# Attention and mixture of experts on one core: a memset one tile later, tables ahead of W2's low parts, another product order and a drain in the half tiles

## Chip, cores and metric

One core of a Trainium2 chip runs the whole program. The metric is device time of one execution in microseconds (us). Before the change the median of three runs is 827.66 us.

## What is computed

Attention with a forget gate (8 batches, 8 heads, 576 positions, 64 numbers a head), whose output is read as 4608 tokens of 512 numbers. Each token then goes to the one of 8 experts that has the largest gate logit:

```python
for e in range(E):
    mask = e_idx == e
    h = np.maximum(x[mask] @ w1[e], 0.0)
    out[mask] = gate_w[mask, None] * (h @ w2[e])
```

W1 is 512x1024 and W2 1024x512 for each expert, all in float32. Which expert a token has is known only on the chip.

## The kernel before, in words

**Two phases.** Attention takes the first 355 us or so; a planner with due times sets its order, and the change doesn't touch it. Its last steps scatter the tokens into a buffer `xs` in DRAM, sorted by expert (indirect DMAs of GpSimd). The expert phase then walks over tiles of `xs`: up to 18 tiles of 256 tokens (`full`, inside `run`), then up to 8 tiles of 128 tokens (`halves`, `half`, `layers_h`), each within an If on a count that is known at run time. In the executions shown here 18 full tiles and 3 half tiles run.

**Which tile comes next.** A tile's expert, its place in `xs` and whether its weights differ from those of the tile ahead are numbers in small integer tables, made by VectorE (DVE) from the token counts. The first four tiles are served by a table made early (`c_taba`). In tile 2 (`t == TABLES`) `other_tables` makes the others: `c_tabb` for the full tiles from the fifth on, `c_tabc` for the half tiles; the last element of each row is written by the CASTs on lines 1123, 1124 and 1130. `self.tabled` holds the names of the last instructions of the tables. The queue of SyncE (SP) reads a row of the table into registers (line 1176) and then issues the loads of that tile: W1 into `raw1` (two DMAs of 1 MB, line 1204, `load_w1`), W2 into `raw2` (two of 1 MB, line 1217, `load_w2`) and the tokens `xg` (line 1196, `load_x`). It does all this in one order, so a row that isn't there yet holds up every load behind it.

**Products in parts.** For accuracy each float32 operand is split: a rounded high part in the type fp32r (`w1h`, `w2h`, `xh`, `hh`), made by ScalarE (ACT), and a low part in bf16, the rest (`w1l`, `w2l`, `xl`, `hl`), made by DVE as original less high part. A product is then three sums: high by high in fp32r, and high by low and low by high in bf16. `products(ks, last, high, *low)` lists them: with `last` true the fp32r products come at the end, else first.

```python
        m = [(k, *x) for x in low for k in ks]
        h = [(k, *high) for k in ks]
        return m + h if last else h + m
```

**A full tile** (`full(t)`) issues the load of the next W1, splits W2 (`split_w2`, lines 1242 and 1243: four quarters of w2h on ACT and of w2l on DVE), loads the next W2, runs layer 1 (`first`), splits the next W1 (`split_w1`, lines 1223 and 1225), turns the next tile's tokens (`prepare`) and runs layer 2 (`second`), whose two halves of 128 tokens are each scaled by DVE into `y` (line 1322) and stored by an indirect DMA of GpSimd (line 1323). In this phase the framework's scheduler sets each engine's order, held only by the data and by `self.order(x, behind)`, which says that x stands behind another instruction on their engine and adds no wait.

**raw1b.** Half tiles use two W1 buffers in turn, `raw1` and `raw1b`. A load is skipped where the expert doesn't change, so GpSimd zeroes `raw1b` (128x4096) once, in tile 3 (`t == TABLES + 1`, line 1490).

**A half tile** (`layers_h`) is written out by hand for TensorE (PE), ACT and DVE (`manual_schedule`): the order in the code is the order on these engines. Layer 2 has 24 products of 128x512 into one bank `py`, in two halves of 12 (i = 0 and 1, four k each). `products` gets i as its `last`: the first half has fp32r first, the second has it last. After the first four products PE turns the second part of h, DVE makes the last quarter of w2l (`quarter_w2(3, False)`, line 1361) and then all four quarters of the next tile's w1l (line 1225). ACT scales the result into `y` (line 1406) and GpSimd stores it (line 1407).

Of the kernel before, what the change touches and what calls it, by code (L numbers as in the profile page):

```python
# [16 lines left out]
I32 = mybir.dt.int32  # L17
# [25 lines left out]
NT = 4608  # L43
# [6 lines left out]
TABLES = 2  # L50
# [17 lines left out]
def upper(ap):  # L68

    n = len(ap.shape)  # L70
    axes = " ".join("abcd"[:n - 1])
    return ap.bitcast(BF16).rearrange(f"{axes} (n two) -> {axes} n two", two=2)[(slice(None),) * n + (1,)]
# [151 lines left out]
class Attn:  # L224
# [741 lines left out]
    def run(self, early, others):  # L966
        self.others = others
        self.own("acc", -1)
        with self.tc.manual_schedule():
            self.setup(*self.begin)  # L970
            for s in self.steps(early).order():
                s["fn"]()
                self.turn_over(BETWEEN.get(s["name"], 0), 256)
# [19 lines left out]
class Moe:  # L993
# [369 lines left out]
    def layers_h(self, t):  # L1363

        nc = self.nc
        xg, xh, xl = self.xgh[t], self.xhh[t], self.xlh[t]
        hb = self.next("hb")
        ph = [self.next("ph") for _ in range(2)]
        m = [self.products(range(4), q, (xh, self.w1h), (upper(xh), self.w1l), (xl, upper(self.w1h))) for q in range(2)]

        def first(q, js):
            for j in js:
                k, x, w = m[q][j]
                nc.tensor.matmul(ph[q], x[:, k, :], w[:, k, q * 512:q * 512 + 512], start=(j == 0), stop=(j == 11))
            if js[-1] == 11:
                nc.scalar.activation(hb[:, q], ph[q], AF.Relu)

        for q in range(2):
            self.quarter_w2(q, True)
            self.quarter_w2(q, False)  # L1380
        first(0, range(12))
        self.quarter_w2(2, True)
        first(1, range(8))
        self.turn_h(hb, 0)
        self.quarter_w2(2, False)
        first(1, range(8, 12))
        self.quarter_w2(3, True)
        if t < 7:
            self.prepare_h(t + 1, "ph")
        py = self.next("py")  # L1390
        m2 = [x for i in range(2) for x in self.products(range(4 * i, 4 * i + 4), i, (self.hh, self.w2h), (upper(self.hh), self.w2l),
                                                         (self.hl, upper(self.w2h)))]

        def second(js):
            for j in js:
                k, h, w = m2[j]
                nc.tensor.matmul(py, h[:, k, 0:P], w[:, k, :], start=(j == 0), stop=(j == len(m2) - 1))

        second(range(4))
        self.turn_h(hb, 1)  # L1400
        self.quarter_w2(3, False)
        if t < 7:
            self.split_w1((t + 1) % 2)
        second(range(4, 24))
        y = self.next("y")
        nc.scalar.activation(y, py, AF.Copy, scale=xg[:, 512:513])
        nc.gpsimd.indirect_dma_start(self.out, bass.IndirectOffsetOnAxis(ap=xg[:, 513:514].bitcast(I32), axis=0), y, None,  # L1407
                                     bounds_check=NT - 1, oob_is_err=False)

    def early(self, acc, pc):  # L1410

# [53 lines left out]
    def run(self, acc, loads, behind, ahead, ranks):  # L1465
        self.load_w1(self.row[0], 0, loads)
        self.load_w2()
        behind = self.split_w1(0, [0], behind, (0, 2))
        behind = self.prepare(0, behind)
        for x in ahead:  # L1470
            self.order(x, behind[1])
        self.split_w1(0, [1, 2, 3], behind, (0, 2))

        def full(t):
            self.load_w1(self.row[t + 1])
            if t + 2 < FULL and t != TABLES:
                self.load_x(t + 2)
            if t == OTHERS:
                self.pads(pc)
            behind = self.split_w2(None if t else ranks)  # L1480
            self.load_w2()
            self.first(t, None if t else ranks, behind)
            self.split_w1(0, behind=(self.relu, behind[3][1]) if t <= OTHERS else None)
            if t + 1 < FULL:
                self.prepare(t + 1, None if t else (behind[3][0], behind[1][1]))
            if t == TABLES:
                self.other_tables(n)
                self.load_x(t + 2)
            if t == TABLES + 1:
                self.order(self.nc.gpsimd.memset(self.raw1[1], 0.0), self.low)  # L1490
            half = self.second(self.xg[t], 2)
            if t == 0:
                self.half_way = half

        for t in range(ALWAYS):
            if t == OTHERS:
                pc = self.px(0)
                n = self.counts(acc, pc, "b", self.half_way)
            full(t)
        nt = self.val(self.row[EARLY], 3, FULL - EARLY, ALWAYS - EARLY, ())  # L1500
        nh = self.val(self.rowh[0], 3, 8, 0, ())
        for h in range(2):
            self.load_xh(h)
        self.prepare_h(0)
        kept = self.kept()
        with self.tc.If(nt >= FULL - EARLY) as most:
            for t in range(ALWAYS, FULL):
                full(t)
            self.halves(nh)
        with most.Else():  # L1510
            self.kept(kept)
            with ExitStack() as nest:
                for t in range(ALWAYS, FULL - 1):
                    nest.enter_context(self.tc.If(nt > t - EARLY))
                    full(t)
            self.halves(nh)
# [92 lines left out]
```

## Time and profile before

| what | us |
|---|---|
| median of three runs | 827.66 |
| the three runs | 827.66, 821.95, 827.77 |
| the profiled execution: its own time | 822.82 |
| the profiled execution: first to last instruction (span) | 820.8 |
| PE busy | 780.6 |
| DVE busy | 622.6 |
| ACT busy | 593.3 |
| GpSimd (POOL) busy | 388.7 |

Times in the views are us from the span's start. A row of the timeline gives start, length, engine, line, operation, what is written and read, how often, and in brackets how long the engine was idle just before and what ended that. An engine name with a q (POOLq, SPq) is that engine's sequencer or DMA queue. A wait is put down to what came last by the profile.

### The profile page before, as it was taken

Reading aid. Unit: us, or ns where it says so; the run is one execution under the profiler, and the core shown is the slowest. Engines: PE = TensorE matmul, PEld = TensorE weight load, DVE = VectorE, ACT = ScalarE, POOL = GpSimd, SP = SyncE. Lnnn points to the kernel's source line nnn. Section 1 sums busy time; section 2 is a strip of 40 time slices with the busy share of each in tenths; the row PEclk is TensorE's granted clock in tenths of the full one; section 3 lists DMA queues with packets and bytes.
Section 4 is the critical chain, followed back from the end, with each engine's and each line's share of the span. In section 5 each row is a group of like instructions: output and inputs, shape, how many; then the busy total and the mean of one; then the engine's idle time right before and its main releaser. Section 6 shows DMA issues by size and latency. Waiting matters only on the chain. (4 is left out here: it accounts for less than half of the span.)

```text
span 820.8 us, 23634 instructions
## 1 busy us (share of the span) xinstructions
PE 780.6 (95%) x9659; PEld 619.1 (75%) x9659; DVE 622.6 (76%) x1178; ACT 593.3 (72%) x799; POOL 388.7 (47%) x376
## 2 busy tenths in 40 slices
PE   8998999999999998899998999999999999999994
PEld 4788888888888887786777777777777767777552
DVE  7888999889898989777887766665656667666494
ACT  5897989798989897685855665655556667666483
POOL 9767989798989886876524011111011010111110
PEclk9999999999999999999999999999999999999998
DMA  5634444445454533262566821101114421115580
GB/s 169 202 118 133 161 150 161 146 139 172 137 172 139 167 115 113 84 235 84 191 208 212 295 72 53 51 27 39 52 53 141 155 67 53 52 62 173 200 294 22
DMA packets 43622, 108.16 MB, mean 132 GB/s; under 512 B 5547, under 2 KB 6123, under 8 KB 43500
## 3 DMA queue, kind: packets, MB, share of 16 engines
q1 hardware_dynamic: 36778, 85.47, 31.2%
q0 software_dynamic: 6704, 21.02, 7.0%
q8 instruction: 80, 1.31, 0.7%
q14 instruction: 42, 0.34, 0.1%
q10 hardware_dynamic: 18, 0.01, 0.0%
HBM read 143.78 MB, written 22.02 MB: 202 GB/s over the span
## 5 line engine op out<-in xcount | busy, mean ns | idle before, releaser
L1323 POOL DMA_INDIRECT out_dram<-y,xg x36 | 50.6, 1405 | 313.1 <-DVE y L1322 286.0
L586 PE MATMUL ps<-X 64*128 64x288 f32 (+5 forms) x1536 | 150.8, 314 | 1.0 <-ACT X L426 1.0
L702 POOL TENSOR_TENSOR Pl<-Pt,Ph 128x1024 f16<-128x1024 f32 (+1 forms) x63 | 142.2, 2264 | 12.9 <-ACT Ph L690 11.6
L1242 ACT CAST w2h<-raw 128x1024 fp32r<-128x1024 f32 x72 | 70.3, 1043 | 86.2 <-PE py L1318 70.4
L1243 DVE TENSOR_TENSOR w2l<-raw,w2h 128x1024 bf16<-128x1024 f32 x72 | 85.0, 1218 | 45.2 <-ACT w2h L1242 45.2
L586 PEld LDWEIGHTS ps<-X 64*128 64x128 f32 (+1 forms) x1536 | 114.3, 181 | 4.0 <-ACT X L426 1.2
L728 PE MATMUL po<-vh,Ph 128*128 128x73 f16 x930 | 101.5, 199 | 3.5 <-DVE lgh L744 3.3
L1225 DVE TENSOR_TENSOR w1l<-raw,w1h 128x1024 bf16<-128x1024 f32 x78 | 96.1, 1243 | 10.8 <-ACT w1h L1223 10.7
L730 PE MATMUL po<-vh,Pl 128*128 128x73 f16 x930 | 101.0, 198 | 1.0 <-DVE Pl L702 1.0
L729 PE MATMUL po<-vl,Ph 128*128 128x72 f16 x930 | 101.3, 197 | 0.0
L1283 PE MATMUL ph<-xh,w1h 128*128 128x256 f32 x576 | 96.3, 299 | 2.7 <-ACT w1h L1223 2.6
L675 ACT ACTIVATE Pt<-ps,lnp 128x576 f32<-128x576 f32 (+1 forms) x96 | 81.6, 865 | 23.4 <-PE ps L586 23.4
L729 PEld LDWEIGHTS <-Ph 128*128 128x128 f16 x960 | 95.1, 99 | 3.0 <-issue 2.9
L728 PEld LDWEIGHTS <-Ph 128*128 128x128 f16 x960 | 94.1, 99 | 4.0 <-DVE lgh L744 1.9
L432 POOL TENSOR_TENSOR X<-raw,X 128x1152 fp32r<-128x1152 f32 x32 | 85.2, 2664 | 24.2 <-ACT X L426 19.7
L730 PEld LDWEIGHTS <-Pl 128*128 128x128 f16 x960 | 94.0, 98 | 1.1 <-DVE Pl L702 1.1
L1318 PE MATMUL py<-w2h,hh 128*128 128x512 f32 x288 | 88.0, 424 | 0.0
L1283 PE MATMUL ph<-xr,w1l 128*128 128x256 bf16 x576 | 87.0, 273 | 0.0
L1283 PE MATMUL ph<-xl,w1h 128*128 128x256 bf16 x576 | 87.0, 274 | 0.0
L1223 ACT CAST w1h<-raw 128x1024 fp32r<-128x1024 f32 x80 | 82.8, 1054 | 4.1 <-DMA raw<-in_w_dram 4.1
L607 DVE TENSOR_REDUCE mt<-ps 128x2 f32<-128x128 f32 (+3 forms) x128 | 81.9, 681 | 3.5 <-PE ps L586 2.6
L1283 PEld LDWEIGHTS ph<-xh,w1h 128*128 128x128 f32 x576 | 77.5, 190 | 7.9 <-ACT w1h L1223 3.1
(307 smaller groups left out, 1699.7 us busy)
## 6 DMA issues: line engine op xcount, KB each, us to landing
raw<-in_w_dram SPq DMA_DIRECT2D x84, 1024.0 KB
raw<-in_qk_dram SPq DMA_DIRECT2D x32, 608.0 KB
vT<-in_vt_dram SPq DMA_DIRECT2D x32, 320.0 KB
xg<-xs SPq DMA_DIRECT2D x18, 514.0 KB
vr<-in_v_dram SPq DMA_DIRECT2D x30, 256.0 KB
raw1b<-in_w_dram SPq DMA_DIRECT2D x4, 1024.0 KB
hxg<-xs SPq DMA_DIRECT2D x5, 257.0 KB
vr<-in_v_dram SPq DMA_DIRECT2D x8, 128.0 KB
```

Source lines behind the costliest of these rows:

```text
L432: e.tensor_tensor(self.two(X[:, 1]), self.two(self.get("raw", p)), self.two(f32(X[:, 0])), ALU.subtract)
L586: self.nc.tensor.matmul(ps[0:m, h, c:c + w], a(r), b(r), start=start, stop=not any(x[0] is ps for x in parts[n + 1:]), skip_group_check=True)
L607: nc.vector.tensor_reduce(mt[:, :, ic:ic + 1], pm[:, :, c0:c0 + w], AX.X, ALU.max)
L702: e.tensor_tensor(self.Pl_t[p % 2][:, :, c], self.exps(p, i), self.Ph_t[p % 2][:, :, c], ALU.subtract)
L728: nc.tensor.matmul(o, Ph[:, c0:c0 + P], vh[:, c, hh, :], start=(c == 0), stop=False)
L729: nc.tensor.matmul(o[:, 1:73], Ph[:, c0:c0 + P], vl[:, c, hh, :], start=False, stop=False)
L730: nc.tensor.matmul(o, Pl[:, c0:c0 + P], vh[:, c, hh, :], start=False, stop=(c == ic))
L1223: x = nc.scalar.copy(self.w1h[a], self.raw1[i][a])
L1225: y = e.tensor_tensor(self.w1l[a], self.raw1[i][a], f32(self.w1h[a]), ALU.subtract)
L1243: y = nc.vector.tensor_tensor(self.w2l[a], self.raw2[a], f32(self.w2h[a]), ALU.subtract)
L1283: y = nc.tensor.matmul(ph[:, i, :], w[:, k, f0:f0 + P], x[:, k, :], start=(j == 0), stop=(j == len(m) - 1))
L1318: x = nc.tensor.matmul(py, h[:, k, c * P:c * P + P], w[:, k, :], start=(j == 0), stop=(j == len(m) - 1))
```

## The change

Four edits. (1) The memset of `raw1b` is issued in tile 4 (`TABLES + 2`) and no longer in tile 3. (2) In tile 3 the four w2l subtractions are ordered behind the last instructions of the tables. (3) In half tiles both halves of layer 2 have their fp32r products first. (4) In half tiles GpSimd gets a `drain` that its order puts ahead of the store.

```diff
@@ layers_h
-        m2 = [x for i in range(2) for x in self.products(range(4 * i, 4 * i + 4), i, (self.hh, self.w2h), (upper(self.hh), self.w2l),
+        m2 = [x for i in range(2) for x in self.products(range(4 * i, 4 * i + 4), 0, (self.hh, self.w2h), (upper(self.hh), self.w2l),
...
-        nc.gpsimd.indirect_dma_start(self.out, bass.IndirectOffsetOnAxis(ap=xg[:, 513:514].bitcast(I32), axis=0), y, None,
-                                     bounds_check=NT - 1, oob_is_err=False)
+        d = nc.gpsimd.drain()
+        x = nc.gpsimd.indirect_dma_start(self.out, bass.IndirectOffsetOnAxis(ap=xg[:, 513:514].bitcast(I32), axis=0), y, None,
+                                         bounds_check=NT - 1, oob_is_err=False)
+        self.order(x, d.ins.name)
@@ run, full(t)
-            behind = self.split_w2(None if t else ranks)
+            behind = self.split_w2(None if t else ranks, self.tabled if t == TABLES + 1 else ())
...
-            if t == TABLES + 1:
+            if t == TABLES + 2:
                 self.order(self.nc.gpsimd.memset(self.raw1[1], 0.0), self.low)
```

On DVE, between the last y of tile 2 (`y_9392`, line 1322) and layer 1 of tile 3, a minus is before and a plus now:

```order
 L1168 SCALAR_TENSOR_TENSOR c_eb<-c_okb,c_ec,c_eb 1x15
-L1243 TENSOR_TENSOR w2l<-raw_9378,w2h 128x1024 x2
 L1123 CAST c_tabb<-c_eb 1x15
 L1129 TENSOR_TENSOR c_chb<-c_eb 1x15
-L1243 TENSOR_TENSOR w2l<-raw_9378,w2h 128x1024 x2
-L1289 SCALAR_TENSOR_TENSOR hl<-ph_9349,hh 128x512
 L1130 CAST c_tabb<-c_chb 1x15
-L1289 SCALAR_TENSOR_TENSOR hl<-ph_9350,hh 128x512
+L1243 TENSOR_TENSOR w2l<-raw_9378,w2h 128x1024 x4
+L1289 SCALAR_TENSOR_TENSOR hl<-ph_9349,hh 128x512
```

The three small instructions of the table stood between the quarters of w2l and behind a hl; now they come first and the four quarters of w2l follow in one run. On GpSimd's queue the memset stood behind the second store of tile 2 and stands behind the second store of tile 3.

On PE, in the first half tile, at the turn from the first to the second half of layer 2 and at its end (`hh`, `hl` high and low part of h; lines between are the same):

```order
 L1397 MATMUL py_9354<-w2h,hl 128x512
+L1397 MATMUL py_9354<-w2h,hh 128x512 x4
 L1397 LDWEIGHTS hh
 L1397 MATMUL py_9354<-w2l,hh 128x512
...
 L1397 MATMUL py_9354<-w2h,hl 128x512
-L1397 MATMUL py_9354<-w2h,hh 128x512 x4
```

Four fp32r products went from the end of the second half to its start; the bf16 products by w2l come four products later. On PE, in the full tile 13 (counted from 0), where its layer 2 opens before the last quarter of its layer 1 (`px` the turned tokens of the next tile, `py` the results):

```order
+L1263 MATMUL px_9344<-cident,xg_63 128x128 x4
 L1263 MATMUL px_9359<-cident,xg_63 128x128 x4
-L1318 MATMUL py_9354<-w2h,hh 128x512 x2
-L1318 LDWEIGHTS hr
-L1318 MATMUL py_9355<-w2l,hr 128x512
-L1318 LDWEIGHTS hr
-L1318 MATMUL py_9355<-w2l,hr 128x512
-L1318 MATMUL py_9354<-w2h,hh 128x512 x2
```

The scheduler gave the full tiles 5 to 13 another interleave: where fp32r and bf16 products stood in pairs by turns, there is now one fp32r product. Counted over these nine tiles the order has 70 changes from fp32r to bf16 before and 45 now, with the same products; tiles 15 and 16, which are the same in both, have 6 each, and tiles 10 and 11 had 8 each before.

## Rows read from the trace of the kernel before

**Rows 1.** The page's part 1: busy us, share of the span, instructions.
```profile
PE 780.6 (95%) x9659; PEld 619.1 (75%) x9659; DVE 622.6 (76%) x1178; ACT 593.3 (72%) x799; POOL 388.7 (47%) x376
```
**Rows 2.** Windows of 30 us, PE alone: us, busy, granted clock, DMA share, GB/s.
```profile
430.00:460.00 30.00, 27.36 (x195) 1.00 0.72 256
...
760.00:790.00 30.00, 29.44 (x142) 1.00 0.60 219
```
**Rows 3.** Waits of PE, whole span: us in total, times, longest.
```profile
PE ph L1283 <- ACT w1h L1223: 2.6, 1, 2.6
...
PE py L1397 <- DVE w2l L1361: 1.8, 3, 0.6
```
**Rows 4.** Timeline from 428 to 447 us, engine by engine.
```profile
446.97 0.51 PE L1283 MATMUL ph<-xh,w1h 128*128 128x256 f32 x2 [2.64 <-ACT w1h L1223]
...
445.88 1.99 ACT L1223 CAST w1h<-raw 128x1024 fp32r<-128x1024 f32 x2 [4.10 <-DMA raw<-in_w_dram]
...
440.63 1.10 SPq L1204 DMA_DIRECT2D raw<-in_w_dram  x2
...
430.63 0.21 DVE L1168 SCALAR_TENSOR_TENSOR c_eb<-c_okb,c_ec,c_eb 1x15 f32<-1x15 f32 x1
...
436.07 3.90 DVE L1130 CAST c_tabb<-c_chb 1x15 int32<-1x15 f32 x1
...
436.39 3.56 POOL L1490 MEMSET raw1b<- 128x4096 f32 x1
```
**Rows 5.** Windows of 2 us: us, granted clock, DMA share, GB/s.
```profile
438.00:440.00 2.00, 1.00 0.00 0
...
444.00:446.00 2.00, 1.00 1.04 400
```
**Rows 6.** Timeline of the first half tile's layer 2, PE and DVE.
```profile
779.82 0.59 PE L1397 MATMUL py<-w2l,hh 128*128 128x512 bf16 x2
780.97 0.59 PE L1397 MATMUL py<-w2l,hh 128*128 128x512 bf16 x2 [0.56 <-DVE w2l L1361]
...
783.22 0.39 PE L1374 MATMUL ph<-w1h,hxh 128*128 128x512 f32 x1
...
779.70 1.21 DVE L1361 TENSOR_TENSOR w2l<-raw,w2h 128x1024 bf16<-128x1024 f32 x1
```
**Rows 7.** Timeline of the last half tile's end, DVE, ACT and POOL.
```profile
806.59 4.62 DVE L1225 TENSOR_TENSOR w1l<-raw1b,w1h 128x1024 bf16<-128x1024 f32 x4
...
809.18 0.69 ACT L1406 ACTIVATE y<-py,hxg 128x512 f32<-128x512 f32 x1 [0.69 <-PE py L1397]
...
784.38 1.94 POOL L1407 DMA_INDIRECT out_dram<-y,hxg  x1 [11.04 <-ACT y L1406]
...
810.14 1.93 POOL L1407 DMA_INDIRECT out_dram<-y,hxg  x1 [10.96 <-ACTq L1526]
```
**Rows 8.** Line 1605, the program's end: ns min/median/max, first and last start.
```profile
L1605 POOLq DRAIN  x3: 51/107/7276, 812.7 to 820.5; - x3
L1605 SPq DRAIN  x3: 7/7/13, 815.3 to 820.2; - x3
```
**Rows 9.** GpSimd's indirect DMAs: count, ns min/median/max, first and last start.
```profile
L836 POOL DMA_INDIRECT xs<-x,rde x40: 915/988/1966, 92.1 to 384.1; - x40
...
L1188 POOL DMA_INDIRECT xs<-c_nobody,c_at x8: 962/1139/1960, 398.5 to 409.6; - x8
...
L1323 POOL DMA_INDIRECT out_dram<-y,xg x36: 984/996/4712, 385.3 to 771.6; - x36
```
**Rows 10.** PE timeline, the last run of products of four full tiles.
```profile
590.54 2.20 PE L1318 MATMUL py<-w2h,hh 128*128 128x512 f32 x8
...
635.65 2.19 PE L1318 MATMUL py<-w2h,hh 128*128 128x512 f32 x8
...
701.70 2.20 PE L1318 MATMUL py<-w2h,hh 128*128 128x512 f32 x8
746.70 2.21 PE L1318 MATMUL py<-w2h,hh 128*128 128x512 f32 x8
```

## The prediction, made before the changed kernel ran

> **What bounds the kernel now.** I read the page's busy line first: PE works 780.6 of 820.8 us [rows 1], so nothing else can be worth much unless it stops PE or lies behind PE's end. Next the windows of PE, to find where it is not full in the expert phase: between 430 and 460 us it lacks 2.64 us, between 760 and 790 us 0.56 us [rows 2]; in the windows between these it is full. The list of PE's waits names both: one of 2.6 us for w1h, and three, 1.8 us in all, for w2l in the half tiles [rows 3]. Then the timelines of these places, and last the rows of the program's end, which no busy share shows: after the last store GpSimd sits in one DRAIN of 7.28 us [rows 8].
>
> The profiled execution took 822.82 us, 2.0 more than its span. The median of the three runs is 827.66, and the three stand at two levels, 822 and 827.7, some 5 us apart; the profile shows one of the lower level, and nothing in one trace says what the other is made of. My sum is made against 822.82; 827.66 less 822.82 is 4.84, which I add for the median's level.
>
> **Edits 1 and 2: the memset and the tables.** The PE wait at 446.97 is for w1h of tile 4; ACT waited for the W1 data, whose load SP issued at 440.63, and the cast began 5.25 us later [rows 4]. SP could not issue it earlier because the row of c_tabb wasn't complete: its last CAST (one partition, 15 numbers) began at 436.07 and took 3.90 us, until the memset's end (436.39 and 3.56, so 439.95) [rows 4]. Two things made it late: four w2l between it and the table's other instructions, and the memset beside it. In the new order the three small instructions follow c_eb, which ended at 430.84 [rows 4], at once, and the memset isn't near. I put the row at 431.2 and SP's load at 432, 8.6 us earlier than 440.63. The DMA engines are free then (0 GB/s as late as 438 to 440, against 400 in 444 to 446) [rows 5], so the data are there near 437.3 by the same 5.25 us, and PE needs w1h at 444.3. The wait of 2.6 us goes. What is late next: nothing I can see; PE then follows its own products. Term: -2.6, bounds -2.6 and 0.
>
> What edit 2 delays are four w2l, by three instructions as small as c_eb with its 0.21 us [rows 4]; PE reads w2l much later. The memset in its new place stands behind the second store of tile 3, while DVE works on w2l, hl and w1l of tile 4. No row shows it beside these. If they wait as the CAST did, DVE loses up to 3.56 us; DVE is 76% busy [rows 1], and the bound for PE is 0 to +2.6 (3.56 less a microsecond of slack, an estimate). I take 0 because hl and xl read PSUM and the row beside it is a cast, another operation; rival B is the other end. The move past SP's queue costs nothing, since SP's order is unchanged. The stores behind the memset wait for y far later.
>
> **Edit 3: products of the half tiles.** PE stops 0.56 us before the third w2l product, because DVE's last w2l began at 779.70 and took 1.21 us [rows 6]. The twelve products take from 779.82 to 783.22 with that wait [rows 6], so 0.24 each without it. With four fp32r products ahead the third w2l product is the seventh and comes at 779.82 and 6 by 0.24, 781.25, after 780.91 when that w2l ends. The wait is covered in all three tiles: 1.8 us in total [rows 3], 0.6 each. One more change from fp32r to bf16 a tile costs 0.03 by the price below, so nothing. The next tile starts 0.6 earlier; I see no other wait of PE in these tiles that would show an engine on the verge of being late.
>
> In the last half tile the gain reaches the end through the store. Its y starts at 809.18, the store at 810.14 and takes 1.93 [rows 7], so it ends at 812.07, 0.86 behind the end of DVE's four w1l (806.59 and 4.62, so 811.21) [rows 7]. The first and the last of the three stores of half tiles take the same [rows 7], while the shortest in full tiles takes 0.98 [rows 9]. So I read it thus: the store gets its turn where one w1l ends and the next begins. Those seams are 1.15 apart (4.62 by four), at 810.05 too. A store that starts 0.6 earlier, at 809.54, meets that seam and ends one w1l sooner: -1.15 in place of -0.6. Term: 2 by -0.6 and -1.15, so -2.3; bounds -2.4 and -1.2 (the store still ends with the w1l).
> The Trainium skill (SBUF — State Buffer, section Who interferes with whom) infers that a tensor_tensor on DVE doesn't hold up the writing of descriptors by GpSimd. By that the last store would win only 0.6 and the sum would be 0.55 smaller; the rows above, 1.93 beside w1l, speak against it.
>
> **The interleave of the full tiles.** It isn't among the edits but follows from them. Tiles 10 and 11 together take 45.11 us (590.54 to 635.65), tiles 15 and 16, with the same products and 4 changes of type fewer, 45.00 (701.70 to 746.70) [rows 10]: 0.028 a change. 25 changes fewer in nine tiles: -0.7, bounds -1.5 and 0 (it could be the order and not the changes).
>
> **Edit 4: the drain.** Cost first. Each new drain runs where GpSimd is idle anyway: 11 us ahead of each store of a half tile [rows 7]. Below 10 us it delays nothing. Now what it may give. At the end the first of three DRAINs of GpSimd must be the long one: it starts at 812.7 and 7.28 us later, at 819.98, the others follow; SP reached its own drain at 815.3 and so had seen every store landed [rows 8]. So GpSimd alone keeps the program open for 4.7 us. What takes 7.28 us there is not the last store, which landed before 815.3. It may be what 87 indirect DMAs since the start (40, 8, 36 and the 3 of the half tiles [rows 7, 9]) left to be tidied up, 0.084 each; there was no drain in between. Then the first new drain does nearly all of it in GpSimd's idle time, the last finds one store, and the end comes by SP's 815.3: -4.6. Or each drain after a store costs the same 7.28: then 0. No row has a drain behind a few DMAs only, so these are the two bounds. I take -4.6, since the landed data leave little else for it to wait for, but hardly above even chance.
>
> **Sum.** -2.6 - 2.3 - 0.7 - 4.6 = -10.2: 812.6 at the profile's level, 817.5 at the median's.
>
> **Rivals.**
> A: the last drain is as long as before, because its length belongs to any drain behind a store. For it: 7.28 us is a long time for bookkeeping that could have been done in idle time. Then -5.6: 822.1 at the median's level, 817.2 at the profile's.
> B: the memset holds DVE in tile 4 as it held the CAST, and what edit 1 wins is lost a tile later: +2.6. For it the CAST's 3.90 us; against it that DVE's work there has slack and other operations. 820.1.
> The Trainium skill (same page and section) says that a two-input operation from SBUF contends only with GpSimd work that reads SBUF, and a memset only writes; by that rule B falls. No row here shows that pair.
> C, slower: the drains in the half tiles run beside DVE's w1l and w2l, and as the stores there take 1.93 and not 0.98, a drain too may take twice its 7.28 there, 14.6 us, each time. The point from which this decides is the 11 us of idle time. From GpSimd's last store of the full tiles (done at 773.3, 11.04 before 784.38 [rows 7]) three rounds of 14.6 and 1.93 end the last store at 822.9 in place of 812.07; with the 3.3 of edits 1, 2 and the interleave taken off, and the last drain as now, +7.5: 835.2. Against it: the idle time would have had to be just too short, and if the backlog theory holds only the first drain is long.
>
> **How the numbers follow.** Forecast 0.50, A 0.36, B 0.10, C 0.04. The predicted time is the forecast's, 817.5. Each case can come at either level, about as likely, since the runs stand two to one and the profiled one at the lower. The forecast spans 812.6 to 817.5, A 817.2 to 822.1, B 815 to 820. With a microsecond at each end for the bounds the range is 811.8 to 823.2; C and about a tenth of the others lie outside. About 1% is what a measurement of this kernel can tell from no change: 8.3 us, so faster means under 819.4. That holds for the forecast but a tenth (0.45), for A at the lower level (0.16) and a little of B: 0.62. Slower needs over 835.9, the upper side of C and what I haven't seen: 0.03. The rest is 0.35.
>
> **What would show it.** Edits 1 and 2: line 1130's CAST as short as its neighbours, SP's W1 load near 432, PE full between 430 and 460. Edit 3: no wait of PE for w2l in half tiles; the last store about 1 us long. Interleave: tiles 5 to 13 a tenth shorter each. Edit 4: POOLq's new DRAINs, the first long, the last short, and the span's end within a microsecond of SP's drain. It is wrong if the last DRAIN keeps its 7 us (A), if hl or w1l of tile 4 takes 3 us beside the memset (B), or if a store of a half tile starts after its y by more than 0.5 us (C).

## The result, and the profile after

| what | before, us | after, us |
|---|---|---|
| median of six runs each | 824.18 | 814.12 |
| lowest and highest of the six | 821.95, 827.77 | 813.42, 818.33 |
| profiled execution: its own time | 822.82 | 813.55 |
| profiled execution: span | 820.8 | 811.8 |

The ratio after to before is 0.988, 95% interval 0.9846 to 0.9914: faster by about ten microseconds. The forecast was 817.5 in 811.8 to 823.2. The profile of the changed kernel answers the steps one by one. First the page's busy line (columns as in [rows 1]) and the windows of PE (as in [rows 2]):

```profile
PE 780.1 (96%) x9659; PEld 619.9 (76%) x9659; DVE 618.5 (76%) x1178; ACT 593.5 (73%) x799; POOL 385.1 (47%) x376
```
```profile
430.00:460.00 30.00, 30.00 (x221) 1.00 0.78 272
760.00:790.00 30.00, 29.88 (x146) 1.00 0.61 217
```

PE does the same work as before, 780.1 against 780.6 us [rows 1]; both gaps of [rows 2] are closed. The 0.12 us that is missing in the second window is a small new wait, and a later one of the same kind stands in the list of PE's waits, which has no row for w1h (line 1223) and none for w2l (line 1361) any more:

```profile
PE ph L1374 <- DVE w1l L1225: 0.2, 1, 0.2
```

The timeline from 430 to 440 us shows why the first gap closed:

```profile
430.43 0.16 DVE L1130 CAST c_tabb<-c_chb 1x15 int32<-1x15 f32 x1
...
430.51 4.63 DVE L1243 TENSOR_TENSOR w2l<-raw,w2h 128x1024 bf16<-128x1024 f32 x4
...
431.30 1.10 SPq L1204 DMA_DIRECT2D raw<-in_w_dram  x2
...
437.97 1.99 ACT L1223 CAST w1h<-raw 128x1024 fp32r<-128x1024 f32 x2 [2.17 <-DMA raw<-in_w_dram]
```

The CAST takes 0.16 us in place of 3.90 [rows 4], SP's load is issued at 431.30 in place of 440.63 [rows 4], and w1h begins at 437.97 in place of 445.88 [rows 4], while PE is still on tile 3. The memset in its new place, with what DVE does beside it:

```profile
458.45 3.57 POOL L1492 MEMSET raw1b<- 128x4096 f32 x1
...
458.67 0.68 DVE L1289 SCALAR_TENSOR_TENSOR hl<-ph,hh 128x512 bf16<-128x512 f32 x1
459.27 1.22 DVE L1225 TENSOR_TENSOR w1l<-raw,w1h 128x1024 bf16<-128x1024 f32 x1
460.40 0.68 DVE L1289 SCALAR_TENSOR_TENSOR hl<-ph,hh 128x512 bf16<-128x512 f32 x1
461.00 1.22 DVE L1225 TENSOR_TENSOR w1l<-raw,w1h 128x1024 bf16<-128x1024 f32 x1
462.14 0.68 DVE L1289 SCALAR_TENSOR_TENSOR hl<-ph,hh 128x512 bf16<-128x512 f32 x1
462.74 1.21 DVE L1225 TENSOR_TENSOR w1l<-raw,w1h 128x1024 bf16<-128x1024 f32 x1
```

The rows of hl and w1l within the memset (458.45 to 462.02) are as long as those behind it: 0.68 for hl, 1.22 and 1.21 for w1l. The last half tile, to set beside [rows 7]:

```profile
801.70 4.62 DVE L1225 TENSOR_TENSOR w1l<-raw1b,w1h 128x1024 bf16<-128x1024 f32 x4
...
803.53 0.69 ACT L1406 ACTIVATE y<-py,hxg 128x512 f32<-128x512 f32 x1
...
804.49 1.55 POOL L1408 DMA_INDIRECT out_dram<-y,hxg  x1 [10.91 <-ACTq L1528]
```

The store takes 1.55 in place of 1.93 and ends at 806.04, before DVE's w1l train (806.32) and no longer behind it. And the program's end, by the rows of its line (1607, before 1605 [rows 8]), the new drains (line 1407) and the sequencers' rows of the half tiles' Ifs (line 1528; ns min/median/max, first and last start):

```profile
L1607 POOLq DRAIN  x3: 51/107/2604, 807.5 to 811.6; - x3
L1607 SPq DRAIN  x3: 7/7/13, 810.6 to 811.3; - x3
...
L1607 PEldq DRAIN  x2: 8/40/73, 810.9 to 811.3; - x2
...
L1407 POOLq DRAIN  x3: 3879/6758/8826, 767.4 to 792.1; - x3
...
L1528 PEldq COMPARE_BRANCH  x5: 65/68/4889, 762.3 to 806.0; - x5
...
L1528 POOLq INC_SWDGE_SEM  x1: 226/226/226, 804.9 to 804.9; - x1
```

The last long DRAIN is 2.60 us where it was 7.28 [rows 8]. The three new ones, 8.83, 6.76 and 3.88 us in the trace's order, lie in GpSimd's idle time: each store still starts 0.95 to 0.96 us after the start of its y.

To compare kernels I cut each span into stages: a full tile ends with the last of the eight fp32r products that close it (as in [rows 10]; in after, tile 3 has `451.47 2.20`, so it ends at 453.67), the half tiles with PE's last product, and the tail is from there to the span's end. All lengths are in us.

| kernel (times of profiled execution) | span | to the end of tile 2 | tile 3 | tiles 4 to 13 | 14 to 17 | half tiles | tail |
|---|---|---|---|---|---|---|---|
| before | 820.8 | 429.93 | 27.70 | 223.31 | 89.62 | 38.58 | 11.67 |
| after | 811.8 | 429.20 | 24.47 | 223.22 | 89.62 | 36.98 | 8.35 |
| edit1 | 817.6 | 429.69 | 24.78 | 223.31 | 89.62 | 38.58 | 11.67 |
| edit2 | 822.6 | 435.02 | 24.47 | 223.22 | 89.62 | 38.61 | 11.67 |
| edits12 | 819.8 | 432.20 | 24.47 | 223.22 | 89.62 | 38.61 | 11.67 |
| edit3 | 823.8 | 431.00 | 31.23 | 223.31 | 89.62 | 37.00 | 11.67 |
| no_drain | 818.2 | 432.20 | 24.47 | 223.22 | 89.62 | 36.98 | 11.67 |
| drain_only | 819.1 | 432.14 | 27.60 | 223.31 | 89.63 | 38.60 | 7.85 |
| drain_mid | 820.6 | 434.51 | 24.62 | 223.22 | 89.62 | 36.98 | 11.67 |
| drain_each | 815.0 | 432.49 | 24.47 | 223.22 | 89.62 | 36.98 | 8.20 |
| drain_first | 811.5 | 429.07 | 24.47 | 223.22 | 89.62 | 36.99 | 8.10 |
| mid_anchored | 810.9 | 428.31 | 24.47 | 223.22 | 89.62 | 36.98 | 8.29 |

Read the columns, not the rows. Wherever its code is the same, a stage repeats to 0.03 us, with these exceptions: tile 3 in the old order (27.60, 27.70 and 31.23), drain_mid's tile 3 (24.62), and the tail of the kernels with drains (7.85 to 8.35). What differs most from run to run is the first column, mostly attention (428.31 to 435.02), in which no edit stands but the drains that drain_mid and drain_each have at the program's start. So one profile settles most stages to a tenth of a microsecond, while medians of whole runs need an interval of 3 us to either side. The span's 9.0 us are: attention -0.73 (chance), tile 3 -3.23, tiles 4 to 13 -0.09, half tiles -1.60, tail -3.32.

### The profile page after: what moved, and what is told of

It is laid out like the page before. It is cut to its first block, busy times and chain, and to the rows that moved or that the text cites. A ratio compares the mean times of both kernels' runs of the same rounds, so it can differ in the third digit from the quotient of the medians.

```text
span 811.8 us, 23639 instructions
## 1 busy us (share of the span) xinstructions
PE 780.1 (96%) x9659; PEld 619.9 (76%) x9659; DVE 618.5 (76%) x1178; ACT 593.5 (73%) x799; POOL 385.1 (47%) x376
## 4 chain that ended last, share of the span: by engine, by line
PE 63%; DVE 19%; POOL 8%; ACT 5%; issue 4%; DMA 0%; DVEq 0%; ACTq 0%; POOLq 0%
PE py L1318 24%; PE ph L1283 23%; PE ps L586 5%; POOL Pl L702 4%; DVE mt L607 3%; DVE vl L554 3%; POOL X L432 3%; PE po L728 2%; DVE w1l L1225 2%; PE px L1263 2%; PE po L730 2%; DVE x L741 2%; PE po L729 2%; DVE Pl L702 1%; PE ph L1374 1%
## 5 line engine op out<-in xcount | busy, mean ns | idle before, releaser
L1323 POOL DMA_INDIRECT out_dram<-y,xg x36 | 48.1, 1335 | 312.3 <-DVE y L1322 288.3
L1283 PE MATMUL ph<-xh,w1h 128*128 128x256 f32 x576 | 94.6, 297 | 0.0
L1318 PE MATMUL py<-w2h,hh 128*128 128x512 f32 x288 | 84.4, 417 | 0.5 <-ACT hh L1285 0.3
```

Of the source, the lines that this page charges most:

```text
L1283: y = nc.tensor.matmul(ph[:, i, :], w[:, k, f0:f0 + P], x[:, k, :], start=(j == 0), stop=(j == len(m) - 1))
L1318: x = nc.tensor.matmul(py, h[:, k, c * P:c * P + P], w[:, k, :], start=(j == 0), stop=(j == len(m) - 1))
```

## Experiments

**Edits 1 and 2, apart and together.** The theory: the memset held the CAST, and the w2l ahead of it made it later; which of the two counts?

edit1 is before with this alone:
```diff
-            if t == TABLES + 1:
+            if t == TABLES + 2:
                 self.order(self.nc.gpsimd.memset(self.raw1[1], 0.0), self.low)
```


> The kernel before with the memset a tile later alone; the tables still stand between the quarters of w2l. Theory A, either edit is enough: the CAST on line 1130 is short, ends before 437, SP issues W1's load near 437 instead of 440.6, the data are there near 442.5 and PE waits under 0.5 us instead of 2.64. Theory B, both are needed: the CAST is held by the store's descriptors until after the w2l, and PE still waits 1 us or more. The interleave stays as before (8 changes of type a tile).

Measured: 819.70 us in one run. PE's wait for w1h is gone, tile 3 takes 24.78. The CAST stands where it stood, behind four w2l and an hl, but takes 0.33 (it ends at 436.16, with the store of tile 2 that runs beside it from 431.70 for 4.46), and SP's load follows at 436.82. That is only just soon enough: the first quarter of w1h ends at 443.67 and PE's first product with it starts at 443.74; in the changed kernel they stand at 439.02 and 443.28.
```profile
435.83 0.33 DVE L1130 CAST c_tabb<-c_chb 1x15 int32<-1x15 f32 x1
...
436.82 1.10 SPq L1204 DMA_DIRECT2D raw<-in_w_dram  x2
```

edit2 is before with this alone:
```diff
-            behind = self.split_w2(None if t else ranks)
+            behind = self.split_w2(None if t else ranks, self.tabled if t == TABLES + 1 else ())
```


> The kernel before with w2l behind the tables alone; the memset stays in tile 3, now beside w2l and hl. Theory A: the table is complete at 430.6, SP's load comes near 431.3, PE doesn't wait. The memset runs some time in 432 to 437 beside w2l or hl, which keep their 1.2 and 0.7 us. Theory C, the memset holds w2l and hl as it held the CAST: one of these takes 3 us more and PE waits in tile 3 or 4. The new interleave comes with this edit (5 changes of type), so tiles 5 to 13 take 22.51 us each.

Measured: 824.61 us in one run (its attention was long, 435.02). The wait is gone too, tile 3 takes 24.47. The timeline has the memset still in tile 3, now beside two-input DVE work:
```profile
436.25 0.16 DVE L1130 CAST c_tabb<-c_chb 1x15 int32<-1x15 f32 x1
436.33 4.63 DVE L1243 TENSOR_TENSOR w2l<-raw,w2h 128x1024 bf16<-128x1024 f32 x4
440.87 1.47 DVE L1289 SCALAR_TENSOR_TENSOR hl<-ph,hh 128x512 bf16<-128x512 f32 x2
...
437.37 1.04 POOL L1323 DMA_INDIRECT out_dram<-y,xg  x1 [4.39 <-DVE c_tabb L1130]
438.39 3.56 POOL L1490 MEMSET raw1b<- 128x4096 f32 x1
```
The four w2l take 4.63 with the memset beside them and 4.63 without it in the changed kernel. So a memset held the CAST in before, and here (438.39 to 441.95) it holds no two-input subtraction. The Trainium skill (SBUF — State Buffer, section Who interferes with whom) says that a DVE operation with two inputs from SBUF contends with GpSimd work that reads SBUF and not with one that only writes; these rows agree.

edits12 has both.


> The kernel before with edits 1 and 2 (memset a tile later, w2l behind the tables), half tiles as before. Theory: PE's wait of 2.64 us for w1h of tile 4 is gone, tiles 5 to 13 take the new interleave (5 changes of type a tile); from the last products of tile 2 to those of tile 13 the time is 3.3 us shorter, as with the whole change; PE's three waits in half tiles (1.8 us) and the last DRAIN of 7.3 us stay. Span near 817.5.

Measured: 821.30 us against 824.32, ratio 0.9955 (0.9923 to 0.9987). Tile 3 and tiles 4 to 13 as in edit2. What follows: either edit alone removed the wait, each in one profile (-2.92 us by edit1); edit1 has no margin for tables that come later than they did there. Edit 2 adds the other interleave of the full tiles (edit1 has the old one): from the end of tile 2 to that of tile 13 edit2 takes 247.69 and edit1 248.09, so the order is worth 0.40. Only this sum can be compared: PE's order differs from tile 3 on, not from tile 5, and 169 of PE's rows end in tile 3's stage in edit2, 172 in edit1.

**Edit 3 alone.** before with:
```diff
-        m2 = [x for i in range(2) for x in self.products(range(4 * i, 4 * i + 4), i, (self.hh, self.w2h), (upper(self.hh), self.w2l),
+        m2 = [x for i in range(2) for x in self.products(range(4 * i, 4 * i + 4), 0, (self.hh, self.w2h), (upper(self.hh), self.w2l),
```


> The kernel before with the fp32r products first in both halves of layer 2 of the half tiles alone. Theory: PE's three waits for w2l (0.56, 0.63, 0.61) are gone, PE's last product ends 1.6 us earlier against the last products of the full tiles; the last store starts 0.6 earlier against DVE's w1l and ends one seam sooner; the last DRAIN keeps 7.3 us and follows the store, so the span is some 2 us shorter. Rival: the store still ends with DVE's last w1l and the end moves by 1.2 only.

Measured: 825.59 us against 824.32, ratio 0.9991 (0.9958 to 1.0023): by the time alone nothing can be said of a gain of 2 us. The stages can: half tiles 37.00 against 38.58, the tail 11.67 as before. The profiled run shows something else, in tile 3, which edit 3 doesn't touch: 31.23 us. The timeline from 430 to 453 us:
```profile
434.14 5.43 POOL L1323 DMA_INDIRECT out_dram<-y,xg  x1 [2.73 <-DVE c_eb L1168]
439.56 3.56 POOL L1490 MEMSET raw1b<- 128x4096 f32 x1
...
439.25 3.90 DVE L1130 CAST c_tabb<-c_chb 1x15 int32<-1x15 f32 x1
...
450.15 1.23 PE L1283 MATMUL ph<-xh,w1h 128*128 128x256 f32 x4 [4.74 <-ACT w1h L1223]
```
and PE's windows there (us, busy, granted clock, DMA share, GB/s):
```profile
449.90:453.30 3.40, 3.15 (x14) 0.50 1.04 400
```
The wait is 4.74 us and not 2.64 [rows 3, 4], and when PE resumes its granted clock is 0.50 (1.2 GHz, not 2.4) until 453.3. The same wait so cost 31.23 - 24.78 = 6.5 us here, against 2.9 in the profile on which I predicted. The reason lies further up. In tile 2 DVE's third w1l waited for its data, which it hardly did in before (0.24 us at 417.63), and the tables stand behind it on DVE:
```profile
422.12 1.23 DVE L1225 TENSOR_TENSOR w1l<-raw,w1h 128x1024 bf16<-128x1024 f32 x1 [4.25 <-ACT w1h L1223]
...
436.37 2.34 DVE L1243 TENSOR_TENSOR w2l<-raw,w2h 128x1024 bf16<-128x1024 f32 x2
```
The same w2l and the store of before's trace:
```profile
433.20 2.34 DVE L1243 TENSOR_TENSOR w2l<-raw,w2h 128x1024 bf16<-128x1024 f32 x2
...
431.70 4.71 POOL L1323 DMA_INDIRECT out_dram<-y,xg  x1 [3.80 <-DVE c_eb L1168]
```
The last of the four w2l ends 7.71 us behind the end of tile 2 here and 5.61 in before; in both traces the store ends 0.86 to 0.87 behind it, the memset queues behind the store and holds the CAST. These 2.10 us are the whole difference of the two waits (4.74 and 2.64); the store's greater length (5.43, against 4.71) makes none of it. Another 1.4 of the 3.5 us between 6.5 and 2.9 are left; PE ran at the slower clock for 3.4 us there, but what that alone cost was not separated. Why W1's data came late in tile 2 of this run, and how often they do, isn't shown.

**The drains.** Three theories stand in the expectations, under changing numbers. Backlog: a drain costs 0.084 us for each indirect DMA since the last drain. Fixed cost: each drain behind a store takes long. No part of the drains: the time belongs to the program's end, or to the place where the last store ends among DVE's w1l. A store's landing is here the last update of its DMA's semaphore in the trace.

no_drain is the change without edit 4.


> The changed kernel without the drains (edits 1 to 3 alone). Theory 1, backlog: the last DRAIN of GpSimd is again some 7.3 us long (2.6 with the change), GpSimd keeps the program open, and from the end of PE's last product to the span's end it is 11 to 11.7 us as before (8.3 with the change); the span is some 3 us longer than the changed kernel's 811.8, the time near 817. Theory 2, the drains have nothing to do with it and the last DRAIN got short since the last store now ends at another seam of DVE's w1l: the last DRAIN is 2.6 us here too and the end is 8.3 us behind PE.

Measured: 819.85 us against 828.28, ratio 0.9913 (0.9875 to 0.995). The long DRAIN is back, and so is the tail of 11.67. Beside it stands a row that I had overlooked:
```profile
L1605 POOLq DRAIN  x3: 51/107/7277, 810.0 to 817.9; - x3
```
```profile
L1526 POOLq INC_SWDGE_SEM  x1: 1942/1942/1942, 807.6 to 807.6; - x1
```
GpSimd's sequencer updates a semaphore for 1.94 us, beside the last store, before it gets to the DRAIN; in after that row takes 0.23. The store ends where the changed kernel's does (2.55 behind PE's end), so its place among w1l isn't what shortens the last DRAIN.

drain_only is before with edit 4 alone.


> The kernel before with the drain ahead of the half tiles' stores and nothing else. Theory 1, backlog: the last DRAIN falls to 2 to 3 us, the first new one is the longest (about 7 behind the store ahead of it), end 8.3 us behind PE's last product, time some 3.3 us under before. Theory 2: the last DRAIN keeps 7.3 us and the time doesn't change.

Measured: 820.77 us against 828.28, ratio 0.9934 (0.9899 to 0.9969); the tail is 7.85, so the drains alone are worth 3.82.

drain_mid was to put one drain in the middle of the full tiles, in place of those in the half tiles:
```diff
+            d = nc.gpsimd.drain() if c == 0 and self.mid else None
...
+            if d is not None:
+                self.order(x, d.ins.name)
```


> The changed kernel with one single drain, ahead of the first store of full tile 9, and none in the half tiles. It leaves 20 indirect DMAs behind it (17 stores of full tiles and 3 of half tiles) of 87. Theory 1, backlog by count: from 7.28 us for 87 and 2.6 for one, each DMA costs 0.054 us over a fixed 2.5; the last DRAIN takes about 3.6 us, the one in the middle about 6 (67 DMAs). Theory 3, a drain has a long fixed cost whenever stores are behind it and only shortens when the one ahead of it was just before: the last DRAIN is 6 to 7.3 us.

Measured: 822.44 us in one run, tail 11.67. The experiment missed its aim: the drain stands ahead of the store but behind nothing, and the scheduler put it at the program's start, ahead of all indirect DMAs:
```profile
L1323 POOLq DRAIN  x1: 537/537/537, 3.8 to 3.8; - x1
```
drain_each has the same line for the full tiles from the sixth on, beside the drains of the half tiles.


> The changed kernel with a drain ahead of every store from full tile 5 on, so that nearly all drains have one store behind them. Theory 1: the first takes about 6 us, all others some 2.5 us, with those beside DVE's w1l and w2l longer; the last DRAIN 2.6 and the end as in the changed kernel, 8.3 us behind PE; the drains in full tiles delay stores but no other engine, so the time is the changed kernel's. Theory 3: drains keep 4 us and more, and second stores of full tiles come late by 2 us and more, still off PE's path.

Measured: 816.68 us in one run, tail 8.20. Its 26 drains of full tiles were bunched too, 18 at the start, with GpSimd's first work beside them and no indirect DMA ahead, the others from 682 us on. The first of the latter found 76 indirect DMAs and took 6.47 us, 6.29 of them behind the end of the store that it met; those right behind a drain took 0.03 to 0.04:
```profile
L1323 POOLq DRAIN  x26: 34/416/6473, 1.4 to 688.9; - x26
```
A long drain far from the end speaks against the theory of the program's end. Against the fixed cost speak the drains that find a single store: in after, drain_only and drain_each there are nine, the last DRAINs among them, and each ends 0.07 to 0.09 us behind that store's landing, after 1.30 to 7.38 us.

drain_first keeps only the first of the change's three drains.
```diff
-        d = nc.gpsimd.drain()
+        d = nc.gpsimd.drain() if t == 0 else None
```


> The change with the drain ahead of the first half tile's store only (none ahead of the other two). Backlog theory, as the earlier runs sized it (0.084 us for each indirect DMA since the last drain): the first drain takes about 7 us for 84 DMAs, the last DRAIN of the program finds three, 0.25 us of backlog, and so lasts only until some 2 us behind the landing of the last store, 2 to 3 us as in the change. From PE's end to the span's end 8.0 to 8.6 us (the change 8.35, without drains 11.67). If it were the drain of the tile just before that shortens the last one, or if every store wanted its own, the last DRAIN would be longer than 4 us and the end at 9.5 or more.

Measured: 813.38 us in one run. The tail is 8.10, in the forecast range. The last DRAIN is longer than I wrote, 4.71, but only because it starts earlier, while the store is still running; it ends 6.58 us behind PE's end, the changed kernel's 6.57.

mid_anchored is no_drain with one drain in tile 9, held behind the last store of tile 8:
```diff
+            d = nc.gpsimd.drain() if c == 0 and self.mid else None
+            if d is not None:
+                self.order(d, self.stored)
...
+            if d is not None:
+                self.order(x, d.ins.name)
```


> The change without drains in the half tiles, but with one drain in full tile 9 (counted from 0), held behind the last store of tile 8, so that the scheduler can't bring it forward as it did in drain_mid. Backlog theory: 66 indirect DMAs are behind this drain, 5.5 us; 21 are left for the last DRAIN, 1.75 us, less than the 2 us or so that it waits for the last landing, so 2 to 3 us if the two run side by side, some 4 if they add; from PE's end to the span's end 8.0 to 8.6 in the first case, up to 10 in the second. Theory that the last DRAIN belongs to the stores of the half tiles or to the branch into them: 7.28 and 11.67 as without drains. The rest as in the change without drains: tile 3's stage 24.47, half tiles 36.98.

Measured: 812.82 us in one run, tail 8.29:
```profile
L1323 POOLq DRAIN  x1: 7420/7420/7420, 566.1 to 566.1; - x1
```
```profile
L1611 POOLq DRAIN  x3: 51/112/5206, 804.8 to 810.6; - x3
L1611 SPq DRAIN  x3: 7/7/13, 809.8 to 810.3; - x3
```
```profile
L1532 POOLq INC_SWDGE_SEM  x1: 622/622/622, 803.7 to 803.7; - x1
```
The drain began at 566.12 beside the last store of tile 8 (566.35 and 1.71) and ended 5.47 behind it, where 66 times 0.084 gives 5.5. So one drain, here or in the first half tile, takes the backlog away, and three are not needed. With 21 DMAs left the last DRAIN ended 7.44 us behind PE's end, with 1 and 3 left 6.57 and 6.58, with 87 left 10.83. My expectation left the choice between "side by side" and "add" open; the measured 0.87 for the 18 DMAs more lies between none and 18 by 0.084, 1.5.

The long drains so fit one number, counted from the end of the store that a drain met: 5.47 us for 66, 6.29 for 76, 6.95 for 84 (drain_first's), 7.28 for 87 (the last DRAIN of before, which begins behind the store), which are 0.083, 0.083, 0.083 and 0.084 each. The backlog theory stands for them. All these DMAs have 128 rows, so whether the cost goes by DMA or by row isn't shown. The semaphore update grows as well: 0.23, 0.27, 0.62 and 1.94 us with 1, 3, 21 and 87 DMAs behind, 0.2 and 0.02 for each. With few DMAs behind it the last DRAIN waits for the last store's landing: in after it ends at 810.06 and the landing is at 809.99, so 0.07 behind, and as much in drain_only and drain_each. With 3 DMAs (drain_first) it ends 0.17 behind the landing, with 21 (mid_anchored) 0.90, so a small backlog is in part done by then.

None of these kernels beats the changed one by more than a run's chance: drain_first's 813.38 and mid_anchored's 812.82 stand against six runs from 813.42 to 818.33, and the three kernels' tails differ by no more than 0.25 us.

## Why the prediction was right, and where it was not

**Edits 1 and 2, -2.6 forecast, -2.92 measured.** The mechanism was right in each link (load at 432 forecast, 431.30 measured; CAST short; PE full). "Two things made it late" holds only in part: edit1 leaves the four w2l ahead of the CAST, loads at 436.82 and loses nothing in its run, but with a margin of 0.07 us. With tables 2.1 us later, as in edit3's run, edit1 alone would leave PE some 2 us of wait (an estimate from these rows), while the changed kernel has 4.3 us in hand. And the term is not a constant of before: 2.9 in its profile, 6.5 in edit3's.

**The interleave, -0.7 forecast, -0.40 measured.** Edit 2 does bring it about, and its sign was right; 0.028 for a change of type was too much by nearly half (0.40 by 25 is 0.016), within the bounds of -1.5 and 0. Whether the changes of type or the order make it wasn't separated. Two tiles of after that answer to tiles 10 and 11 of [rows 10] (PE's timeline):
```profile
585.60 2.19 PE L1318 MATMUL py<-w2h,hh 128*128 128x512 f32 x8
...
630.63 2.19 PE L1318 MATMUL py<-w2h,hh 128*128 128x512 f32 x8
```
They take 45.03, and 45.11 before; tiles 15 and 16, from which I priced, take 45.00.

**Edit 3, -2.3 forecast, -1.60 measured.** That the wait for w2l goes is right. Two steps of the term were not. "0.6 each": 38.58 - 36.98 is 1.60 for three tiles. By PE's last product of each tile the gain is 0.69, 0.49 and 0.42 (the waits were 0.56, 0.63 and 0.61), since PE, now earlier, meets the end of DVE's four w1l in the second and third tile and waits 0.12 and 0.18:
```profile
776.77 4.62 DVE L1225 TENSOR_TENSOR w1l<-raw1b,w1h 128x1024 bf16<-128x1024 f32 x4
...
781.45 1.02 PE L1374 MATMUL ph<-w1l,hxh 128*128 128x512 bf16 x4
...
793.91 1.02 PE L1374 MATMUL ph<-w1l,hxh 128*128 128x512 bf16 x4 [0.18 <-DVE w1l L1225]
```
"I see no other wait that would show an engine on the verge of being late" was the sentence that failed. And the last store did end one w1l sooner, as forecast: in the frame of that train 1.15 earlier, and 2.55 behind PE's end where it was 2.93. But nothing waited for it: edit3 and no_drain have the shorter store and still the tail of 11.67. Beside the store GpSimd's sequencer updates a semaphore for 1.94 us, from 1.14 to 3.08 behind PE's end in before, in edit3 and in no_drain alike, and the DRAIN starts at 3.55 in all three. That row stood in before's trace too:
```profile
L1526 POOLq INC_SWDGE_SEM  x1: 1942/1942/1942, 810.3 to 810.3; - x1
```
I priced the store's end without asking what ended last behind it.

The half tiles confirm the reading of the store among w1l: a store that starts in a w2l or w1l of DVE ends 0.86 us behind the end of a subtraction, in after behind the third (805.18 and 0.86 are 806.04, the store's end), in before behind the fourth. The twelve traces have 321 indirect DMAs that start so, and the distance is 0.77 to 0.90 in all of them. The Trainium skill (SBUF — State Buffer, Who interferes with whom) infers that tensor_tensor doesn't hold up descriptor writing; here it does, by up to 4.5 us (5.43 against 0.98).

**Edit 4, -4.6 forecast, -3.3 measured.** The backlog theory, held at hardly above even chance, was right and even its 0.084. "The end comes by SP's 815.3" was not: that is 6.15 behind PE's end in before, and it took for granted that SP and all others would be as early. In after SP's first drain stands 7.13 behind PE's end and PE's own at 7.44: PE's sequencer is busy with two branches of the Ifs, 3.92 us from 801.84 and 4.89 from 805.98, so until 810.87, later behind PE's end than before (3.36 from 806.78 and 4.64 from 810.36, until 815.0, which is 5.9 behind). SP is later because it waits for the last store, which lands 6.49 behind PE's end in after (809.99) and 5.52 in before (814.66); SP's drain follows 0.63 behind the landing in both. The order of the rows says that PE's DRAIN (810.93) releases GpSimd's second one (811.21); in mid_anchored it is GpSimd's own (ended 810.03, second at 810.25). With the drain out of the way PE's and SP's sequencers and GpSimd end within about a microsecond, and this is the 1.3 us by which the term was too large: 0.98 for SP and 0.29 for PE behind it. Part of it comes with edit 3. The landing is 6.32 to 6.68 behind PE's end in the kernels that have it and 5.52 to 6.09 in the others, and edit 3 gives 1.60 without drains but 1.12 on top of them (drain_only's 38.60 and 7.85 against 36.98 and 8.35). Why the store lands later was not found, and whether shorter branches would give anything back was not tried.

**Rivals.** A (the drain keeps its 7 us) is false: 2.60. B (the memset holds DVE in tile 4) is false: 0.68 and 1.22 beside it, in two places. C (drains beside w1l so long that stores are late) is false, though the drains are long there: the second took 6.76 with one store behind it, because it ended only when that store had landed (786.15, 0.08 us before the drain's end), in a time in which W's loads were running. But it was over at 786.2, and the first at 776.2, 6.0 and 3.4 us ahead of the next stores.

**The level.** The sum was -10.2 and the profiled executions differ by 822.82 - 813.55 = 9.27, of which 0.73 is attention's chance. By the stages the change itself gave 8.2 us, so that the two medians lie 10.06 apart, as near to 10.2 as they do, is in part luck: edits 3 and 4 were priced 2.0 too high, and the runs' chance makes up for it. What was wrong by more is the 4.84 added for the median: the six runs of before have their median 1.36 above the profiled one, those of after 0.57. The two "levels" were a reading of three numbers. After's six runs follow PE's mean granted clock: 813.55 at 0.996, 813.42 and 813.63 at 0.995, 814.62 and 816.07 at 0.993, 818.33 at 0.989; the profiles show stretches at 0.50, nearly all in attention, whose number differs from run to run.

## What to carry to other kernels

When a term of a sum ends in "and the program ends sooner", list for every engine and queue when it is done, when the last store lands, and what each does after its last visible row; the gain is the distance to the second latest, measured in the changed order, and small rows of sequencers (branches, semaphore updates) belong on that list. A drain among GpSimd's indirect DMAs cost nothing in idle time here and took its backlog off the program's end, but it must be ordered behind a store as well as ahead of one. And where edits can be read stage by stage in the trace, one profile each separates them that whole times, with a spread of several microseconds, can't.

## What the runs showed of the hardware

- GpSimd's DRAIN took 0.083 to 0.084 us for each indirect DMA since the last drain (66, 76, 84, 87 of them, of 128 rows), 0.03 to 0.04 right behind another drain; the semaphore update at the end of the Ifs 0.02 for each and 0.2 besides (1, 3, 21 and 87 of them).
- A drain that found one store of a half tile ended 0.07 to 0.09 us behind that store's landing (nine times in after, drain_only and drain_each).
- An indirect DMA of GpSimd that came among DVE's two-input subtractions ended 0.86 us behind one of them (0.77 to 0.90 in 321 rows), mostly the next, and up to the fourth: it took up to 5.43 us in place of 0.98.
- PE resumed at a granted clock of 0.50 after a wait of 4.74 us in edit3's run; after 2.64 us in before's it stayed at 1.00 [rows 2].
